# A scaled channel matmul on one core: store order, chunk sizes, weight halves, a dummy matmul loop and ScalarE as the only reader of PSUM

## The chip, the cores and the metric

The kernel runs on one core of one Trainium2 chip. The metric is device time in microseconds (us) of one execution, lower is better. Five runs of the kernel before gave 586.42 to 587.04 us, median 586.71. One more execution was taken with the hardware profiler; it took 586.91 us, and its profile covers a span of 585.1 us from the first to the last instruction.

## The reference

```python
def reference(x, dw, pw):            # x: 1 x 384 x 384 x 384 bf16; dw: 1 x 1 x 384; pw: 384 x 384
    out = x * dw[0, 0][None, None, None, :]          # k = 1: no neighbours are summed
    return jnp.einsum('bhwc,cd->bhwd', out, pw)
```

With a 1 x 1 depthwise kernel this is a single product: 147,456 pixels, each a row of 384 channels, times a 384 x 384 matrix whose rows have been scaled by `dw`. 113 MB of x are read and 113 MB of output are written, all in bf16.

## The kernel before

**Units of work.** A *supertile* is 512 pixels; there are 288 (`NS`). Supertiles are loaded and stored in *chunks* of 1 to 8 (`LMAX`), whose sizes `_chunks` (L18) lays down: 1, 1, 2, 4, then thirty-four times 8, then 4, 2, 1, 1. One supertile is 384 KB (393,216 bytes) each way; below this is called a *unit* of transfer. Three X buffers (`NX`) and three O buffers (`NO`) hold chunks in turn; T (transposed x) and PS (a PSUM tile of four banks) alternate between two buffers, by even and odd supertile.

**The steps of one supertile jj**, each on its own engine, with semaphores written out by hand:

- VectorE (DVE) turns x so that channels lie on partitions, in two 32 x 32 block transposes over uint32 (L174), one for each half of the channels. It reads x as uint32, so that two channels travel together; the weights are laid out in even and odd channels to match. From the third supertile on, each half waits until TensorE is done with the same half of supertile jj-2 (`s_pe`).
- TensorE (PE) runs 48 matmuls (L134): six blocks b of 64 channels, for each the even and the odd channel (`par`), for each four row groups q of 32 partitions, which run side by side. Call the four of one (b, par) a *group*: 12 groups to a supertile, six to each half. The first group waits for the transposes (`s_t`) and for both readers of that PSUM tile two supertiles earlier: `s_a` (ScalarE) on q = 0 and `s_d` (VectorE) on q = 3. The first group of the second half waits for the second transpose. The code is a loop of 144 rounds (L150), two supertiles to a round.
- PSUM is emptied into O as bf16 by two engines: VectorE takes the fourth bank (L212) and ScalarE (ACT) the first three (L215).

VectorE's order is: cast of jj, then the two transposes of jj+2, and so on.

**The queue of transfers.** Nearly all DMAs are issued by SyncE (SP), strictly in order: for each chunk t first the load of chunk t+3 (L95), which waits until the transposes of chunk t are done with the X buffer, then the store of chunk t (L105 to L107), which waits for both casts of its last supertile. The first eviction of a chunk waits until the store of three chunks before has left its O buffer (L210, L211).

**Before the first matmul.** SyncE and ScalarE load `pw` in four copies of 288 KB, one for each group of 32 partitions (L89). `dw` is cast by VectorE (`dwsel`, L186). Then twelve pieces w_r = pw_r times dw are made, six on VectorE (L197) and six on ScalarE (L199), and TensorE waits for all twelve (L149). VectorE transposes supertile 0 ahead of its six and supertile 1 behind them.

Of the kernel before, what the change touches and what calls it, by code (L numbers as in the profile page):

```python
# [7 lines left out]
BF16 = mybir.dt.bfloat16  # L8
F32 = mybir.dt.float32
U32 = mybir.dt.uint32  # L10
COPY = mybir.ActivationFunctionType.Copy

LMAX = 8
NX = 3
NO = 3


def _chunks(n_super: int):  # L18

    head, tail = [1, 1, 2, 4], [4, 2, 1, 1]  # L20
    mid = n_super - sum(head) - sum(tail)
    assert mid > 0 and mid % LMAX == 0
    return head + [LMAX] * (mid // LMAX) + tail
# [3 lines left out]
def kernel(  # L27
# [11 lines left out]
    nc = tc.nc  # L39
    P = nc.NUM_PARTITIONS  # L40
    B, H, W, C = x.shape
    assert dw.shape[0] == 1 and dw.shape[1] == 1, "only k=1 depthwise supported"
    D = pw.shape[1]
    N = B * H * W
    assert C == 384 and D == 384 and N % 1024 == 0
    NB = C // 64

    xf = x.rearrange("b h w c -> (b h w) c")
    of = out.rearrange("b h w d -> (b h w) d")

    NS = N // 512
    chunks = _chunks(NS)
    NT = len(chunks)
    s0 = [sum(chunks[:t]) for t in range(NT)]

    consts = ctx.enter_context(tc.tile_pool(name="consts", bufs=1))
# [3 lines left out]
    pw_r = consts.tile([P, NB, 2, D], BF16, name="pw_r")  # L60
    w_r = consts.tile([P, NB, 2, D], BF16, name="w_r")
    dwt = consts.tile([32, NB, 2], BF16, name="dwt")
    dwsel = consts.tile([P, NB * 2], F32, name="dwsel")
    warm = consts.tile([P, 3], F32, name="warm")
    seed = consts.tile([P, 2], F32, name="seed")

    Xs = [bufp.tile([P, 4 * LMAX, C], BF16, name=f"X{i}") for i in range(NX)]
    Ts = [bufp.tile([P, NB, 256], BF16, name=f"T{i}") for i in range(2)]
    Os = [bufp.tile([P, 4 * LMAX * D], BF16, name=f"O{i}") for i in range(NO)]
# [3 lines left out]
    s_t = [[nc.alloc_semaphore(f"s_t{i}{h}") for h in range(2)] for i in range(2)]  # L73
    s_pe = nc.alloc_semaphore("s_pe")
    s_a = [nc.alloc_semaphore(f"s_a{i}") for i in range(2)]
    s_d = [nc.alloc_semaphore(f"s_d{i}") for i in range(2)]
    s_o = [nc.alloc_semaphore(f"s_o{i}") for i in range(NO)]
    s_dw = nc.alloc_semaphore("s_dw")
    s_pw = nc.alloc_semaphore("s_pw")
    s_ds = nc.alloc_semaphore("s_ds")  # L80
    s_wr = nc.alloc_semaphore("s_wr")
    s_seed = nc.alloc_semaphore("s_seed")

    with tc.tile_critical():  # L84
        pw_v = pw.rearrange("(b w r) d -> w b (r d)", w=32, r=2)
        dw_v = dw.rearrange("a e (b w r) -> w (a e b) r", w=32, r=2)

        def load_pw(eng, q):
            eng.dma_start(pw_r[32 * q : 32 * q + 32].rearrange("w b r d -> w b (r d)"), pw_v).then_inc(s_pw, 16)  # L89

        def load_x(t):
            L = chunks[t]
            r = 512 * s0[t]
            src = xf[r : r + 512 * L, :].rearrange("(p s) c -> p (s c)", p=P)
            d = nc.sync.dma_start(Xs[t % NX][:, : 4 * L, :].rearrange("p s c -> p (s c)"), src)  # L95
            if t >= NX:
                je = s0[t - NX] + chunks[t - NX] - 1
                d._wait_ge(s_t[je % 2][1], je // 2 + 1)
            d.then_inc(s_x[t % NX], 16)

        def store(t):
            L = chunks[t]
            r = 512 * s0[t]
            je = s0[t] + L - 1
            nc.sync.wait_ge(s_d[je % 2], je // 2 + 2)  # L105
            dst = of[r : r + 512 * L, :].rearrange("(q p j) d -> p q (j d)", q=4, p=P)
            d = nc.sync.dma_start(dst, Os[t % NO][:, : 4 * L * D].rearrange("p (q e) -> p q e", q=4))  # L107
            d._wait_ge(s_a[je % 2], je // 2 + 2)
            d.then_inc(s_o[t % NO], 16)


        nc.scalar.dma_start(dwt[:], dw_v).then_inc(s_dw, 16)
        load_x(0)
        load_pw(nc.scalar, 2)
        load_pw(nc.sync, 0)
        load_pw(nc.scalar, 3)
        load_pw(nc.sync, 1)
        for t in range(1, NX):
            load_x(t)
        for t in range(NT):  # L120
            if t + NX < NT:
                load_x(t + NX)
            store(t)
        for o in range(NO):
            nc.sync.wait_ge(s_o[o], 16 * len(range(o, NT, NO)))


        def supertile(s, rv):
            for b in range(NB):
                for par in range(2):  # L130
                    for q in range(4):
                        if par == 0 and q == 0 and b in (0, 3):
                            nc.tensor.wait_ge(s_t[s][b // 3], rv)
                        mm = nc.tensor.matmul(  # L134
                            PS[s][:, q, :D],
                            lhsT=Ts[s][32 * q : 32 * q + 32, b, par::2],
                            rhs=w_r[32 * q : 32 * q + 32, b, par, :],
                            start=(b == 0 and par == 0),
                            stop=(b == NB - 1 and par == 1),
                            tile_position=(32 * q, 0),  # L140
                        )
                        if b == 0 and par == 0 and q == 0:
                            mm._wait_ge(s_a[s], rv)
                        elif b == 0 and par == 0 and q == 3:
                            mm._wait_ge(s_d[s], rv)
                        if b in (2, 5) and par == 1 and q == 3:
                            mm.then_inc(s_pe)

        nc.tensor.wait_ge(s_wr, 2 * NB)  # L149
        with nc.tensor.Fori(0, NS // 2, 1) as it:  # L150
            rv = nc.tensor.to_reg(it + 1)
            for s in range(2):
                supertile(s, rv)


        for s in range(2):
            nc.vector.memset(seed[:, s : s + 1], 0.0).then_inc(s_d[s])  # L157
        nc.gpsimd.memset(warm[:], 0.0).then_inc(s_seed)  # L158
        for s in range(2):
            c = nc.scalar.copy(warm[:, s + 1 : s + 2], warm[:, 0:1])  # L160
            if s == 0:
                c._wait_ge(s_seed, 1)
            c.then_inc(s_a[s])

        def transposes(t, j):
            jj = s0[t] + j
            L = chunks[t]
            s = jj % 2
            Xw = Xs[t % NX][:].bitcast(U32)[:, : 4 * L, :].rearrange("p (k l) c -> p k l c", l=L)
            Tw = Ts[s][:].bitcast(U32).rearrange("p b (i k) -> p b k i", k=4)  # L170
            for h in range(2):
                if h == 0 and j == 0:
                    nc.vector.wait_ge(s_x[t % NX], 16 * (t // NX + 1))  # L173
                ins = nc.vector.transpose(  # L174
                    out=Tw[:, 3 * h : 3 * h + 3],
                    in_=Xw[:, :, j, 96 * h : 96 * h + 96].rearrange("p k (b w) -> p b k w", w=32),
                )
                if jj >= 2:
                    ins._wait_ge(s_pe, 2 * (jj - 2) + h + 1)
                ins.then_inc(s_t[s][h])  # L180

        order = [(t, j) for t in range(NT) for j in range(chunks[t])]

        nc.vector.wait_ge(s_dw, 16)
        for q in range(4):
            nc.vector.tensor_copy(  # L186
                dwsel[32 * q : 32 * q + 32, :], dwt[:].rearrange("w b r -> w (b r)")
            ).then_inc(s_ds)
        transposes(*order[0])
        for b in range(NB):  # L190
            for r in range(2):
                eng = nc.vector if r == 0 else nc.scalar
                if b == 0:
                    eng.wait_ge(s_pw, 64)  # L194
                sc = dwsel[:, 2 * b + r : 2 * b + r + 1]
                if r == 0:
                    i = nc.vector.tensor_scalar_mul(w_r[:, b, r, :], pw_r[:, b, r, :], sc)  # L197
                else:
                    i = nc.scalar.activation(w_r[:, b, r, :], pw_r[:, b, r, :], COPY, scale=sc)  # L199
                if b == 0:  # L200
                    i._wait_ge(s_ds, 4)
                i.then_inc(s_wr)
        transposes(*order[1])

        for jj, (t, j) in enumerate(order):
            L = chunks[t]
            s = jj % 2
            Ov = Os[t % NO][:, : 4 * L * D].rearrange("p (q j d) -> p q j d", q=4, d=D)
            if j == 0 and t >= NO:
                nc.vector.wait_ge(s_o[t % NO], 16 * (t // NO))  # L210
                nc.scalar.wait_ge(s_o[t % NO], 16 * (t // NO))  # L211
            e = nc.vector.tensor_copy(Ov[:, 3, j, :], PS[s][:, 3, :D])  # L212
            e._wait_ge(s_pe, 2 * jj + 2)
            e.then_inc(s_d[s])
            a = nc.scalar.copy(Ov[:, 0:3, j, :], PS[s][:, 0:3, :D])  # L215
            a._wait_ge(s_pe, 2 * jj + 2)
            a.then_inc(s_a[s])
            if jj + 2 < NS:
                transposes(*order[jj + 2])


# [28 lines left out]
```

## Time and profile before

| what | us |
|---|---|
| median of five runs | 586.71 |
| profiled execution, and its span | 586.91, 585.1 |
| first matmul starts, last one ends | 13.48, 578.87 |
| PE busy (13,824 matmuls) | 564.1 |
| DVE busy, ACT busy | 563.9, 327.0 |
| longest wait of DVE for x once it runs | 1.6 |
| waits for a store to leave O: DVE, ACT | 2.3, 1.7 |
| bytes moved by DMA | 227.79 MB, mean 389 GB/s |

Times in a profile line are microseconds unless marked ns. A line of the timeline begins with the start and the duration, then engine, source line, operation, out<-in, and in brackets the idle time before it and what ended that. PEld is TensorE's weight load, SPq the part of SyncE that issues DMAs. "DMA" in tenths is the mean busy share of the core's 16 DMA engines in 40 slices of the span.

### The profile page before, as it was taken

How to read it: one execution, taken by the hardware profiler on the slowest of the kernel's cores; microseconds unless marked ns; L12 is line 12 of the kernel's file. 1: busy time of each engine (PE TensorE's matmuls, PEld its weight loads, DVE VectorE, ACT ScalarE, POOL GpSimd, SP SyncE). 2: the span in 40 equal slices, each digit the busy share in tenths (PEclk: the TensorE clock that was granted, in tenths of full speed). 3: DMA queues.
4: the chain of work that ended last, by engine and by line, in shares of the span. 5: the costliest groups of instructions: out<-in, count | busy, mean ns of one | idle time of the engine just before them, and what ended most of it. 6: DMA issues, size and time to landing. Idle time of an engine off the chain costs nothing.

```text
span 585.1 us, 29852 instructions
## 1 busy us (share of the span) xinstructions
PE 564.1 (96%) x13824; PEld 412.9 (71%) x13824; DVE 563.9 (96%) x876; ACT 327.0 (56%) x297; POOL 0.3 (0%) x5
## 2 busy tenths in 40 slices
PE   0999999999999999999999999999999999999995
PEld 0667777777777777777777777777777777777774
DVE  3789999999999999999999999999999999999995
ACT  3455555555555555555555555555555555555553
POOL 0000000000000000000000000000000000000000
PEclk9999999999999999999999999999999999999998
DMA  8799999999999999999999999999999999999858
GB/s 281 253 404 428 427 427 417 405 386 400 403 413 395 389 420 397 380 424 403 386 417 405 404 411 410 393 400 420 387 393 412 399 400 408 399 410 398 330 225 311
DMA packets 29277, 227.79 MB, mean 389 GB/s; under 512 B 1616, under 2 KB 5456, under 8 KB 24656
## 3 DMA queue, kind: packets, MB, share of 16 engines
q1 hardware_dynamic: 28640, 227.09, 96.9%
q10 hardware_dynamic: 624, 0.59, 0.4%
q14 instruction: 12, 0.10, 0.0%
q8 instruction: 1, 0.02, 0.0%
HBM read 114.43 MB, written 113.25 MB: 389 GB/s over the span
## 4 chain that ended last, share of the span: by engine, by line
PE 93%; DMA 5%; ACT 1%; SPq 0%; issue 0%; DVE 0%; ACTq 0%; DVEq 0%
PE ps L134 93%; DMA X<-in_x_dram 2%; DMA pw_r<-in_pw_dram 1%; DMA out_dram<-O 1%; ACT O L215 1%; ACT w_r L199 1%; DVE T L174 0%; SPq L89 0%; SPq L107 0%; SPq L95 0%; SPq L245 0%; DVEq L173 0%; ACTq L211 0%; ACTq L194 0%; SPq L84 0%
## 5 line engine op out<-in xcount | busy, mean ns | idle before, releaser
L134 PE MATMUL ps<-w_r,T 32*128 32x384 bf16 x13824 | 564.1, 322 | 14.8 <-ACT w_r L199 13.5
L134 PEld LDWEIGHTS ps<-w_r,T 32*128 32x128 bf16 x13824 | 412.9, 93 | 165.6 <-issue 15.1
L215 ACT CAST O<-ps 128x1152 bf16<-128x1152 f32 x288 | 322.3, 1119 | 245.5 <-PE ps L134 243.8
L174 DVE STREAM_TRANSPOSE T<-X 128x384 uint32<-128x384 uint32 x576 | 448.0, 850 | 1.7 <-DMA X<-in_x_dram 1.6
L212 DVE CAST O<-ps 128x384 bf16<-128x384 f32 x288 | 160.4, 557 | 7.1 <-PE ps L134 4.8
L199 ACT ACTIVATE w_r<-pw_r,dwsel 128x384 bf16<-128x384 bf16 x6 | 3.1, 602 | 6.1 <-DMA pw_r<-in_pw_dram 6.1
L186 DVE CAST dwsel<-dwt 32x12 f32<-32x12 bf16 x4 | 0.7, 164 | 4.1 <-DMA dwt<-in_dw_dram 4.0
L197 DVE TENSOR_SCALAR w_r<-pw_r,dwsel 128x384 bf16<-128x384 bf16 x6 | 1.5, 313 | 2.6 <-DMA pw_r<-in_pw_dram 2.6
L160 ACT ACT_TABLE_LOAD x1 | 1.3, 1283 | 2.3 <-issue 2.3
L157 DVE MEMSET seed<- 128x1 f32 x2 | 0.1, 59 | 1.0 <-SPq L84 1.0
L160 ACT COPY warm<-warm 128x1 f32<-128x1 f32 x2 | 0.3, 188 | 0.0
L234 POOL MEMSET const-bfloat16-1.0<- 128x1 bf16 x1 | 0.1, 102 | 0.0
L234 POOL MEMSET const-uint8-127<- 128x1 uint8 x1 | 0.1, 102 | 0.0
L158 POOL MEMSET warm<- 128x3 f32 x1 | 0.1, 101 | 0.5 <-SPq L84 0.5
L234 POOL MEMSET const-float32-0.0<- 128x1 f32 x1 | 0.1, 99 | 0.2 <-issue 0.2
L234 POOL MEMSET const-float32-1.0<- 128x1 f32 x1 | 0.1, 99 | 0.0
## 6 DMA issues: line engine op xcount, KB each, us to landing
X<-in_x_dram SPq DMA_DIRECT2D x34, 3072.0 KB, 17.8
out_dram<-O SPq DMA_DIRECT2D x34, 3072.0 KB, 23.0
X<-in_x_dram SPq DMA_DIRECT2D x2, 1536.0 KB, 12.4
out_dram<-O SPq DMA_DIRECT2D x2, 1536.0 KB, 13.6
X<-in_x_dram SPq DMA_DIRECT2D x4, 384.0 KB, 5.4
X<-in_x_dram SPq DMA_DIRECT2D x2, 768.0 KB, 10.2
out_dram<-O SPq DMA_DIRECT2D x4, 384.0 KB, 3.9
out_dram<-O SPq DMA_DIRECT2D x2, 768.0 KB, 11.3
```

What stands on the lines that cost most here:

```text
L134: mm = nc.tensor.matmul(PS[s][:, q, :D], lhsT=Ts[s][32 * q : 32 * q + 32, b, par::2], rhs=w_r[32 * q : 32 * q + 32, b, par, :], start=(b = ...
L157: nc.vector.memset(seed[:, s : s + 1], 0.0).then_inc(s_d[s])
L158: nc.gpsimd.memset(warm[:], 0.0).then_inc(s_seed)
L160: c = nc.scalar.copy(warm[:, s + 1 : s + 2], warm[:, 0:1])
L174: ins = nc.vector.transpose(out=Tw[:, 3 * h : 3 * h + 3], in_=Xw[:, :, j, 96 * h : 96 * h + 96].rearrange("p k (b w) -> p b k w", w=32),)
L186: nc.vector.tensor_copy(dwsel[32 * q : 32 * q + 32, :], dwt[:].rearrange("w b r -> w (b r)")).then_inc(s_ds)
L197: i = nc.vector.tensor_scalar_mul(w_r[:, b, r, :], pw_r[:, b, r, :], sc)
L199: i = nc.scalar.activation(w_r[:, b, r, :], pw_r[:, b, r, :], COPY, scale=sc)
L212: e = nc.vector.tensor_copy(Ov[:, 3, j, :], PS[s][:, 3, :D])
L215: a = nc.scalar.copy(Ov[:, 0:3, j, :], PS[s][:, 0:3, :D])
L234: nc = _bacc.Bacc("TRN2", target_bir_lowering=False, num_devices=1)
```

## The change

It does six things.

1. Chunk sizes: 1, 1, 2, 2, 3, 3, 4, then thirty-two times 8, then 6, 4, 3, 2, 1 (44 chunks where there were 42).
2. In every chunk of 8 with an even number, SyncE issues the store of chunk t ahead of the load of chunk t+3; elsewhere the order stays.
3. `pw` comes in eight copies of half the size, first those of blocks 0 to 2 for all four row groups, then those of blocks 3 to 5, each half with a semaphore of its own. ScalarE casts `dwsel`; VectorE makes nine of the twelve w_r pieces and ScalarE three, and TensorE waits for each piece just ahead of its use. These waits stand in the loop body, in the even supertile only: 11 groups, in all 144 rounds.
4. TensorE first runs a loop of 11 times 8 matmuls on zeros that GpSimd has written.
5. ScalarE alone empties PSUM, all four banks in one instruction. `s_d` and its waits are gone from TensorE and from the stores.
6. The last supertile is emptied by both engines, two banks each, and stored in two halves, one issued by SyncE and one by ScalarE.

```diff
-    head, tail = [1, 1, 2, 4], [4, 2, 1, 1]
+    head, tail = [1, 1, 2, 2, 3, 3, 4], [6, 4, 3, 2, 1]
...
-        def load_pw(eng, q):
-            eng.dma_start(pw_r[32 * q : 32 * q + 32].rearrange("w b r d -> w b (r d)"), pw_v).then_inc(s_pw, 16)
+        def load_pw(eng, q, h):
+            bs = slice(3 * h, 3 * h + 3)
+            eng.dma_start(
+                pw_r[32 * q : 32 * q + 32, bs].rearrange("w b r d -> w b (r d)"), pw_v[:, bs]
+            ).then_inc(s_pw[h], 16)
...
-        load_pw(nc.scalar, 2)
-        load_pw(nc.sync, 0)
-        load_pw(nc.scalar, 3)
-        load_pw(nc.sync, 1)
+        for h in range(2):
+            for q in range(2):
+                load_pw(nc.scalar, 2 + q, h)
+                load_pw(nc.sync, q, h)
...
-        for t in range(NT):
+        for t in range(NT - 1):
+            late = chunks[t] == LMAX and t % 2 == 0
+            if late:
+                store(t)
             if t + NX < NT:
                 load_x(t + NX)
-            store(t)
+            if not late:
+                store(t)
+        nc.sync.dma_start(of_last[:, 2:4], o_last[:, 2:4])._wait_ge(s_d, 1).then_inc(
+            s_last, 16
+        )
...
+        wr_eng = {(b, r): int(r == 1 and b % 2 == 0) for b in range(NB) for r in range(2)}
...
                         if b == 0 and par == 0 and q == 0:
                             mm._wait_ge(s_a[s], rv)
-                        elif b == 0 and par == 0 and q == 3:
-                            mm._wait_ge(s_d[s], rv)
+                        elif s == 0 and q == 0:
+                            mm._wait_ge(*wr_done[b, par])
...
-        nc.tensor.wait_ge(s_wr, 2 * NB)
+        nc.tensor.wait_ge(s_zero, 1)
+        with nc.tensor.Fori(0, 11, 1) as _:
+            for i in range(8):
+                nc.tensor.matmul(
+                    PS[1][:, i % 4, :D],
+                    lhsT=zero[32 * (i % 4) : 32 * (i % 4) + 32, 0:P],
+                    rhs=zero[32 * (i % 4) : 32 * (i % 4) + 32, :],
+                    start=True,
+                    stop=True,
+                    tile_position=(32 * (i % 4), 0),
+                )
+        nc.tensor.wait_ge(*wr_done[0, 0])
...
-        nc.vector.wait_ge(s_dw, 16)
+        nc.scalar.wait_ge(s_dw, 16)
...
+        for (b, r), e in wr_eng.items():
+            eng = (nc.vector, nc.scalar)[e]
+            if (e, b // 3) not in first:
+                eng.wait_ge(s_pw[b // 3], 64)
...
+            i.then_inc(s_wr[e])
...
             if j == 0 and t >= NO:
+                nc.scalar.wait_ge(s_o[t % NO], 16 * (t // NO))
+            nq = 4
+            if jj + 1 == NS:
+                nq = 2
                 nc.vector.wait_ge(s_o[t % NO], 16 * (t // NO))
-                nc.scalar.wait_ge(s_o[t % NO], 16 * (t // NO))
-            e = nc.vector.tensor_copy(Ov[:, 3, j, :], PS[s][:, 3, :D])
-            e._wait_ge(s_pe, 2 * jj + 2)
-            e.then_inc(s_d[s])
-            a = nc.scalar.copy(Ov[:, 0:3, j, :], PS[s][:, 0:3, :D])
+                e = nc.vector.tensor_copy(Ov[:, nq:4, j, :], PS[s][:, nq:4, :D])
+                e._wait_ge(s_pe, 2 * jj + 2)
+                e.then_inc(s_d)
+            a = nc.scalar.copy(Ov[:, 0:nq, j, :], PS[s][:, 0:nq, :D])
...
+        nc.scalar.dma_start(of_last[:, 0:2], o_last[:, 0:2])._wait_ge(s_a[(NS - 1) % 2], (NS - 1) // 2 + 2).then_inc(
+            s_last, 16
+        )
```

## The prediction

> **What bounds the kernel now.** I read the page's busy line and DMA line first, then the timeline of one period in mid-stream, then the chain of waits at both ends, then the DMA issues by time.
>
> ```profile
> PE 564.1 (96%) x13824; PEld 412.9 (71%) x13824; DVE 563.9 (96%) x876; ACT 327.0 (56%) x297; POOL 0.3 (0%) x5
> ...
> DMA  8799999999999999999999999999999999999858
> ```
>
> PE, DVE and the DMA engines all look full. The timeline from 301.9 us tells PE and DVE apart:
>
> ```profile
> 302.02 1.12 ACT L215 CAST O<-ps 128x1152 bf16<-128x1152 f32 x1 [0.83 <-PE ps L134]
> 302.02 0.56 DVE L212 CAST O<-ps 128x384 bf16<-128x384 f32 x1
> 302.50 1.55 DVE L174 STREAM_TRANSPOSE T<-X 128x384 uint32<-128x384 uint32 x2
> 303.97 1.12 ACT L215 CAST O<-ps 128x1152 bf16<-128x1152 f32 x1 [0.83 <-PE ps L134]
> ```
>
> A period is 303.97 - 302.02 = 1.95 us. In the matmul records the 12 groups of a supertile start 162 or 163 ns apart, with no wider gap at a supertile's border: 12 x 162.5 = 1950 ns. Both casts start together, released by PE; DVE's second transpose ends at 304.05, when PE has only begun the next supertile, whose second half is due 0.97 us later. So PE sets the pace, 288 x 1.95 = 561.6 us, and DVE's full row costs nothing. Whatever can be gained lies in the other 585.1 - 561.6 = 23.5 us. The chain shows where:
>
> ```profile
> 1.88 8.04 DMA pw_r<-in_pw_dram
> ...
> 10.01 3.15 ACT w_r L199 x6
> ...
> 13.48 4.05 PE ps L134 x48
> ...
> 19.15 12.45 DMA X<-in_x_dram
> ...
> 32.69 538.40 PE ps L134 x13248
> ...
> 572.26 7.45 DMA out_dram<-O
> ...
> 579.79 1.12 ACT O L215
> ```
>
> PE starts at 13.48; its first 14 groups are 320 ns apart (half speed, up to 17.9, where the clock record reaches 1.0), so the third supertile starts at 19.54; x is late by 1.45 us at 32.69; at the end the last cast waits for a store. The DMA engines are a second bound, close behind. This is the landing time of large DMAs at 62 to 110 us, then at 480 to 530 us:
>
> ```profile
> X<-in_x_dram SPq DMA_DIRECT2D x4, 3072.0 KB, 13.9
> out_dram<-O SPq DMA_DIRECT2D x3, 3072.0 KB, 19.2
> ```
> ```profile
> X<-in_x_dram SPq DMA_DIRECT2D x3, 3072.0 KB, 19.6
> out_dram<-O SPq DMA_DIRECT2D x3, 3072.0 KB, 25.0
> ```
>
> A DMA's semaphore is raised 16 times. The first raise stays about 10 us after the issue of a load; only the last grows, from 13.7 to 19.7. One of 16 engines falls behind: its landings are about 7.4 us apart for 8 units loaded and 8.4 for 8 stored, 15.8 in all against the 15.6 that PE takes for a chunk.
>
> **The change part by part**, as time saved or added on the path to the end.
>
> *Weights in halves (3).* In order of issue the four copies land at 6.75, 7.32, 8.82 and 9.92. The first half is the bytes of the first two, so it lands at about 7.3; the second at 9.9. X0 landed at 5.38, so DVE's transposes of supertile 0 end by 7.0. One w_r piece is 0.31 us on DVE, each further 0.245; from w_r to the first matmul took 13.48 - 13.16 = 0.32 us. PE starts at 7.3 + 0.05 + 0.31 + 0.32 = 8.0. Its six groups take 0.97; then it waits: five DVE pieces from 9.95 to 11.25, last group done at about 11.65. DVE's transposes of supertile 1 start at 11.2, the first half is ready at 12.1, PE starts it at 12.15, and the third supertile at 14.1. That is 19.5 - 14.1 = **5.4 us saved**. Between bounds: weights no earlier than now (9.9) leave a start at 10.3, a third supertile at about 14.5 and 5.0 saved; if halves cost as much as whole copies, 1.5 us less. ScalarE's four `dwsel` casts end by about 6, before any weight; its three pieces (0.52 apart) are off the path.
>
> *Dummy loop (4).* 22 groups from about 1.6 us. By the first supertile's rows, 14 at 320 ns and 8 at 162.5 are 5.8 us: done at 7.4, ahead of 8.0. All at half speed they end at 8.6, costing 0.6. Without the warm clock the head loses about 1 us. Both are in the range.
>
> The Trainium skill ("TensorE: Matmul & The Clock Gate", Part 1) gives about 3.4 us to full clock, where this trace took 4.4; its figure would end the loop at about 6.8, still ahead of the weights.
>
> *Small chunks at the head (1).* Now SyncE holds the fourth-next load (issued 19.15) behind the store of supertile 0, and 8 units then land at 31.59. After the change 3 units follow there, issued at about 13.5 and due at about 19.9; a unit takes 0.92, so they land at about 19. The next loads (3, 4, 8 units) have 3 us or more in hand. **1.45 us saved**; at worst half comes back at the first chunk of 8.
>
> *ScalarE alone (5).* 1119 ns for 1152 elements; 384 more at the nearest row's rate (about 0.83 ns) give 1.44 us, under the 1.95 period; PE needs that PSUM tile again 1.95 us after it finished it. Cover left 0.45 us. **0.** If one instruction over four banks took 1.9 us or more, each 0.1 above it would cost 29 us. DVE loses 0.48 us of work that nobody waited for, and frees X about 1 us earlier.
>
> *Eleven more waits (3).* They stand in 144 rounds. Now, the groups that carry waits (first and seventh) are spaced 162.4 to 162.6 ns like the rest, so a satisfied wait costs under 1 ns: **0**, at most 1.6 us.
>
> The Trainium skill ("Advanced Engine Details and Errata", Network/Comms) says that reading a semaphore from the sequencer takes 50 to 100 ns. If PE paid that unhidden, 1584 waits would add 79 to 158 us. The spacing above speaks against it, though only for waits at least 24 matmuls apart.
>
> *Order of transfers (2).* In even chunks the load is issued 3.4 us later and behind 8 units of store. So it lands when the store does now, 25 us after the chunk's last cast; it is needed 28.6 after. Cover 3.6 us, hence **0**; odd chunks keep their place. Fewer changes between reading and writing might help the engines; no row shows it, so -2 to +3 us, taken as 0.
>
> *Tail (1, 6).* Now PE ends at 578.9, the last store lands at 583.77, the span ends 1.36 later. Afterwards the last cast is two banks: DVE 0.16 + 768 x 1.04 ns = 0.96; two issues and hand-overs 0.5; landing 2.4 for half the bytes (2.83 now). The chunk that last used the O buffer is stored 11.7 us before PE's end, not 6.7, so that wait goes. So 3.9 instead of 4.8: **0.9 saved**, if the queue is empty.
>
> It is not quite. With PE 7 us earlier, the slow DMA engine has no idle time from 15 us on. Counting every chunk through one queue at 0.925 us a unit loaded and 1.05 stored, its last bytes land at 577 to 578.4, while PE ends at 571.9 and the tail wants 575.7. Of that excess of 1.3 to 2.7 I take about half, because the 15 other engines are quicker and DVE's halved program needs fewer of the 12 instruction fetches of 8 KB: **1.1 added**; bounds 0 and 2.7.
>
> Sum: 586.9 - 5.4 - 1.45 - 0.9 + 1.1 = 580.2 beside the profiled execution's 586.91; the median of the runs is 0.2 lower: **580.0 us**.
>
> **The rivals.**
> - *The slow DMA engine becomes the bound.* For: 15.8 against 15.6 now, and lag of 10 us at the end. At 0.93 and 1.055 a unit its queue ends at 581.2, x comes late several times near the end (the loads of the last small chunks sit behind stores of 8 units): 581.2 + 1.36 + 1.8 = **584.4**. Against: it has always caught up when demand fell.
> - *The head gains half* (clock falls back in the 1.3 us pause for the second half, or eight copies land later): 580 + 2.5 = **582.5**. Against: after the last matmul the clock stayed at 1.0 for 2.2 us.
> - *Waits in the loop hold PE up*: slower. Place: PE, even supertiles. At 10 ns each, 1584 x 10 ns = 15.8 us: 580 + 15.8 = **596**. It decides from 6.7/1584 = 4.2 ns a wait. For: one wait in every four matmuls is six times as dense as any now. Against: 162.5 ns a group gives cover, and 4 waits a supertile show nothing.
> - *ScalarE's four-bank cast is too slow*: same side, less likely.
>
> **How the numbers follow.** Differences under 0.2% (1.2 us) can't be told from no change. Forecast 0.58 (577.5 to 582), slow engine 0.19, half head 0.10, waits or cast slower 0.09, sums that cancel within 0.2% 0.04. Range 577.3 to 585.0: the low end is a tail without the 1.1 and weights 1.5 us earlier; the high end is the slow-engine case with a bit of the head lost. Faster 0.87, same 0.04, slower 0.09.
>
> **What the profile after would show.** First w_r matmul near 8.0 and third supertile near 14.1; ACT casts of 1.44 us, 1.95 apart in mid-stream (a wider period means waits or casts); no wait for x near 30; last matmul near 572; last loads landing up to 25 us after issue. I would be wrong if the period moved, if halves landed no earlier, or if PE waited for x from 500 us on.

## The result and the profile after

The changed kernel takes a median of 588.75 us against 586.42 us before; the ratio is 1.0036, 95% interval 1.0028 to 1.0045. It is slower by 0.36%, where 580.0 us, 1.1% faster, was forecast, with a range of 577.3 to 585.0. The profiled execution took 588.28 us over a span of 586.5 us (before: 586.91 and 585.1).

The page after, busy times and the group of the transposes, which are now VectorE's only steady work:

```profile
PE 570.8 (97%) x13912; PEld 418.4 (71%) x13912; DVE 496.9 (85%) x586; ACT 417.9 (71%) x298; POOL 0.5 (0%) x6
...
PE 71%; DMA 24%; DVE 2%; ACT 1%; SPq 1%; issue 0%; DVEq 0%
...
L207 DVE STREAM_TRANSPOSE T<-X 128x384 uint32<-128x384 uint32 x576 | 493.8, 875 | 80.1 <-DMA X<-in_x_dram 31.3
L250 ACT CAST O<-ps 128x1536 bf16<-128x1536 f32 x288 | 413.8, 1437 | 157.5 <-PE ps L156 157.5
```

The chain is no longer nearly all PE: 24% of it is DMA. VectorE waits 31.3 us for x, of which 5.4 are the wait for the very first chunk; the kernel before waited 1.6 once it ran. The chain in order of time (start, duration, what) shows two different halves:

```profile
2.84 6.87 DMA pw_r<-in_pw_dram
...
9.73 1.24 DVE w_r L228 x5
...
11.88 310.26 PE ps L156 x7632
...
324.06 28.38 DMA X<-in_x_dram
...
352.54 2.73 DVE T L207 x4
...
355.26 29.11 DMA X<-in_x_dram
...
385.48 31.41 PE ps L156 x768
...
418.81 29.72 DMA X<-in_x_dram
```

Up to 322 us the kernel is ahead of the one before, with an unbroken run of matmuls from 11.88. From then on x comes late in every second chunk, and five loads are on the chain; four of them took 28 to 30 us from issue to landing, the last, of 3 units, 18.5. The first late one, in the timeline:

```profile
351.41 1.44 ACT L250 CAST O<-ps 128x1536 bf16<-128x1536 f32 x1 [0.51 <-PE ps L156]
352.54 5.06 DVE L207 STREAM_TRANSPOSE T<-X 128x384 uint32<-128x384 uint32 x7 [2.20 <-DMA X<-in_x_dram]
353.36 1.44 ACT L250 CAST O<-ps 128x1536 bf16<-128x1536 f32 x1 [0.51 <-PE ps L156]
...
353.55 3.76 PE L156 MATMUL ps<-w_r,T 32*128 32x384 bf16 x88 [0.24 <-DVE T L207]
...
355.73 1.44 ACT L250 CAST O<-ps 128x1536 bf16<-128x1536 f32 x1 [0.93 <-PE ps L156]
```

VectorE stands still for 2.20 us until x lands, and the casts are 355.73 - 353.36 = 2.37 us apart instead of 1.95. From the matmul records, the supertiles longer than 1950 ns, beyond that length, are: 0.42 us at 351, 0.73 at 383, 1.03 at 415, 0.74 at 447, 1.51 at 479, 0.76 at 512, 2.18 at 563; and 0.88 and 0.81 at 567 and 570, where the clock record has fallen to 0.5 for 3.4 us after that pause of 2.2 us. Seven waits cost 7.4 us, the clock 1.7.

The books close: third supertile at 13.83 instead of 19.54 (-5.7), the early wait for x gone (-1.45), waits +7.4, clock +1.7, and from PE's last matmul to the end 5.8 instead of 6.3 us (-0.5). That is +1.4 us, and 586.5 - 585.1 = 1.4.

Why do the loads take so long? Landing times of the 3 MB transfers at 62 to 110 us, then at 300 to 350:

```profile
out_dram<-O SPq DMA_DIRECT2D x3, 3072.0 KB, 14.2
X<-in_x_dram SPq DMA_DIRECT2D x3, 3072.0 KB, 20.9
```
```profile
X<-in_x_dram SPq DMA_DIRECT2D x3, 3072.0 KB, 25.0
out_dram<-O SPq DMA_DIRECT2D x3, 3072.0 KB, 28.1
```

The lines for X mix turned and other loads. A load that is turned behind a store started with 20.9 us, but takes 28.4 by 324 us, where its cover (28.6 from the chunk's last cast) is used up. The first raise of a DMA's semaphore does not move: for the late loads it stays at 16.1 to 16.3 us after the issue, from 100 us to 500. Only the last of the 16 drifts, from 4 us behind the eighth to 14, while the fifteenth stays within 2 us of the eighth. So one DMA engine lags, as before the change, but its lag grows faster.

### The profile page after: what moved, and what is told of

It is laid out like the page before. It is cut to its first block, busy times and chain, and to the rows that moved or that the text cites. A ratio compares the mean times of both kernels' runs of the same rounds, so it can differ in the third digit from the quotient of the medians.

```text
span 586.5 us, 29841 instructions
## 1 busy us (share of the span) xinstructions
PE 570.8 (97%) x13912; PEld 418.4 (71%) x13912; DVE 496.9 (85%) x586; ACT 417.9 (71%) x298; POOL 0.5 (0%) x6
## 4 chain that ended last, share of the span: by engine, by line
PE 71%; DMA 24%; DVE 2%; ACT 1%; SPq 1%; issue 0%; DVEq 0%
PE ps L156 71%; DMA X<-in_x_dram 23%; DVE T L207 1%; DMA pw_r<-in_pw_dram 1%; ACT O L250 1%; SPq L113 0%; SPq L92 0%; DVE w_r L228 0%; DVE O L247 0%; SPq L100 0%; DVEq L206 0%; SPq L283 0%; SPq L86 0%
## 5 line engine op out<-in xcount | busy, mean ns | idle before, releaser
L207 DVE STREAM_TRANSPOSE T<-X 128x384 uint32<-128x384 uint32 x576 | 493.8, 875 | 80.1 <-DMA X<-in_x_dram 31.3
L250 ACT CAST O<-ps 128x1536 bf16<-128x1536 f32 x288 | 413.8, 1437 | 157.5 <-PE ps L156 157.5
L175 PE MATMUL ps<-zero 32*128 32x384 bf16 x88 | 5.5, 423 | 1.4 <-POOL zero L191 1.4
L175 PEld LDWEIGHTS ps<-zero 32*128 32x128 bf16 x88 | 3.0, 117 | 3.5 <-issue 1.6
L230 ACT ACTIVATE w_r<-pw_r,dwsel 128x384 bf16<-128x384 bf16 x3 | 1.7, 610 | 2.6 <-DMA pw_r<-in_pw_dram 2.6
```

The source lines that it names most:

```text
L175: nc.tensor.matmul(PS[1][:, i % 4, :D], lhsT=zero[32 * (i % 4) : 32 * (i % 4) + 32, 0:P], rhs=zero[32 * (i % 4) : 32 * (i % 4) + 32, :], s ...
L207: ins = nc.vector.transpose(out=Tw[:, 3 * h : 3 * h + 3], in_=Xw[:, :, j, 96 * h : 96 * h + 96].rearrange("p k (b w) -> p b k w", w=32),)
L250: a = nc.scalar.copy(Ov[:, 0:nq, j, :], PS[s][:, 0:nq, :D])
```

## The experiments

Three theories stood. **G (grouping):** store, store, load, load in a row makes the lagging engine slower. **L (late load):** the engine is as it was, the turned loads just go out too late. **E:** something else in the change, ScalarE's eviction or the chunk sizes, slows it. "Two chunks" below is the mean time between landings on the lagging engine for 16 units loaded and 16 stored; PE needs 31.2 us for them. "Lag" is the time from the eighth to the sixteenth raise of one DMA's semaphore. All ratios are to the kernel before on the same chip, with their 95% intervals; runs 1 to 4 share one chip, 5 to 8 a second, 9 and 10 a third. Numbers other than times and ratios come from the one profiled execution of each run.

**1. The changed kernel with the old order.**

```diff
-            late = chunks[t] == LMAX and t % 2 == 0
+            late = False
```

> The changed kernel with the old order of transfers in every chunk (load, then store); all else as changed. Theory G (grouping): two stores and then two loads in a row make the lagging DMA engine slower, 32.1 us for two chunks instead of about 31.5; without it the lag stays as in the kernel before, no wait for x after 350 us, 579 to 581.5 us. Theory L (late load): the engine's rate has nothing to do with the order; the loads of even chunks are just issued too late; also 579 to 581.5, but the lagging engine still takes about 32 us for two chunks and the lag still grows past 10 us. Theory E (ScalarE's eviction or the chunk sizes slow the DMA): the lag grows as in the changed kernel and waits for x come, only later; 583 to 587.

Measured: 578.90 us, ratio 0.9877 (0.9862 to 0.9892). No supertile after the second is longer than 1.95 us; two chunks take about 31.4 us; the lag stays at 9 us or less. The landing times at 400 to 500 us:

```profile
out_dram<-O SPq DMA_DIRECT2D x7, 3072.0 KB, 23.1
X<-in_x_dram SPq DMA_DIRECT2D x6, 3072.0 KB, 18.8
```

That is 588.75 - 578.90 = 9.9 us for one line (9.3 by the two ratios), as much as the whole miss of the forecast (588.75 - 580.0 = 8.75). E is out.

**2. Every chunk of 8 with the store first.**

```diff
-            late = chunks[t] == LMAX and t % 2 == 0
+            late = chunks[t] == LMAX
```

> The changed kernel with the store ahead of the load in every chunk of 8, so that stores and loads alternate one by one again, but every load is as late as the late ones are now. Theory G: the lagging engine returns to about 31.5 us for two chunks, a load lands about 25 us after its issue at the end, under its 28.6 us of cover: 579.5 to 582. Theory L: twice as many late loads, so waits for x in every chunk: 590 or more. Theory E: as the changed kernel, 588 to 592.

Measured: 578.62 us, ratio 0.9872 (0.9857 to 0.9887), the shortest median here, though not to be told from run 1. Twice as many late loads, and not one wait for x reaches PE. Landing times at 400 to 500 us:

```profile
out_dram<-O SPq DMA_DIRECT2D x7, 3072.0 KB, 15.4
X<-in_x_dram SPq DMA_DIRECT2D x7, 3072.0 KB, 22.9
```

Two chunks take 31.3 to 31.4 us, the lag is at most 7 us. L is out: a load behind a store is harmless when stores and loads alternate.

**3. The changed kernel with four X buffers.**

```diff
-NX = 3
+NX = 4
```

> The changed kernel with four X buffers instead of three: a load has one more chunk (15.6 us) until it is needed. Theory G: the lag goes on growing by about 0.9 us for two chunks, no wait for x, but at the end the lagging engine still has some 15 us of stores and loads to work off: 581 to 584. Theory L: no waits and no growth, 579 to 581. Theory E: like G.

Measured: 583.75 us, ratio 0.9958 (0.9945 to 0.9972). No wait for x in mid-stream, yet two chunks take 32.1 to 32.3 us and the lag reaches 15.5: the drift is there without the waits. The time itself has another part that no theory named (us in total, times, longest; the profiled execution, at 585.09, was the slowest of five):

```profile
ACT O L250 <- PE ps L156: 148.4, 282, 2.1
...
ACT O L250 <- DMA out_dram<-O: 6.8, 3, 3.1
```

With four buffers the loads run further ahead at the head, so the first stores queue behind 8-unit loads, ScalarE waits there twice for O (2.6 and 3.1 us), and PE loses 5.9 us between 35 and 54 us (about 1.7 of it to 3.4 us at half clock). The third wait for O, at 501 us, costs PE 0.3 us. More cover moved the wait from x to O.

**4. The kernel before with only the order turned.**

```diff
+            late = chunks[t] == LMAX and t % 2 == 0
+            if late:
+                store(t)
             if t + NX < NT:
                 load_x(t + NX)
-            store(t)
+            if not late:
+                store(t)
```

> The kernel before with only the order of transfers turned in every even chunk of 8. Theory G: the lagging engine goes from 31.5 to about 32.1 us for two chunks, loads land over 28 us after issue from about 350 us on, waits for x of about 0.9 us every second chunk: 590 to 595. Theory L: late loads with a lag that grows as before, one or two short waits near the end: 586.5 to 588.5. Theory E: 586 to 587, since nothing else of the change is in.

Measured: 595.83 us, ratio 1.0161 (1.0147 to 1.0174), just over the range of G. Two chunks take 32.3 us, the first wait for x in mid-stream comes at 358 us, then one of about 1.0 us in every second chunk, and one of 3.4 us at 581:

```profile
DVE T L178 <- DMA X<-in_x_dram: 10.8, 7, 3.6
PE ps L138 <- DVE T L178: 9.4, 8, 3.2
```

Price of the order here: 595.83 - 586.01 (before, same chip) = 9.8 us, the same as in experiment 1.

**5. and 6. Smaller chunks: how long may a run one way be?** Chunks of at most 4 with six buffers each, the order turned in 5 and old in 6.

```diff
-LMAX = 8
-NX = 3
-NO = 3
+LMAX = 4
+NX = 6
+NO = 6
...
-    head, tail = [1, 1, 2, 2, 3, 3, 4], [6, 4, 3, 2, 1]
+    head, tail = [1, 1, 2, 2, 3, 3, 4], [4, 4, 3, 2, 2, 1]
```

> The changed kernel with chunks of at most 4 and six X and six O buffers, order still turned in every even full chunk: stores and loads come two by two again, but a run of the same kind is 8 units long, as in the kernel before, not 16. Theory R (what slows the lagging engine is a run of 16 units one way; its lag can grow until it stands half a period behind the others): lag settles near 8 to 10 us, about 31.5 us for 16 units each way, no wait for x, 578 to 580.5 us. Theory P (the pairing itself, two stores and two loads in a row, whatever their size): lag grows on as in the changed kernel, but cover is longer by two small chunks; 581 to 588.

> The same with the old order, so a run one way is 4 units long. Theory R: lag settles at about 4 to 6 us, 578 to 580 us. Theory P: lag as in the kernel before, 10 us at the end, 578 to 580.

Measured: turned 578.98 us (ratio 0.9870, 0.9845 to 0.9896) with a lag of up to 11.6 us; old 583.84 us (0.9956, 0.9927 to 0.9985; single runs 581.6 to 587.0) with a lag of 13 us. The first fits R, with a lag a little over its figure. The second lies outside both theories, which gave 578 to 580, and refutes R as stated: runs of 4 units should have had the least lag and have more than runs of 8 (16 units each way take 31.8 us on the lagging engine in run 6, 31.6 in run 5). In the profile of run 6, of one of its two fastest executions (581.63), no supertile after the first is longer than 1.95 us; what is left over runs after PE's last matmul at 571.5 (end 579.8). So of the sizes tried "a pair is bad" holds for chunks of 8 only, and the length of a run alone does not tell the lag.

**7. and 8. The price of the chunk sizes and of the dummy loop**, both on the version with the old order: in 7 the sizes of the kernel before, in 8 the loop of 11 times 8 matmuls taken out.

```diff
-    head, tail = [1, 1, 2, 2, 3, 3, 4], [6, 4, 3, 2, 1]
+    head, tail = [1, 1, 2, 4], [4, 2, 1, 1]
```

> The changed kernel with the old order and with the old chunk sizes, to price the new sizes alone against the run with the old order (578.9). By the prediction's terms: x of the first chunk of 8 late by about 1.2 us near 24 us, and the last cast waiting for a store near the end by about 0.9: 580 to 582. If the sizes are hidden by other work: 578.5 to 579.5.

> The changed kernel with the old order and without the dummy matmul loop. By the rows of the first supertile before (320 ns a group for 4.4 us), the second half of supertile 0 and a little of supertile 1 run at half speed: third supertile at 14.4 to 14.8 instead of 14.0, 579.3 to 580. If the pauses for the weights keep the clock down longer: third supertile at 16 or later, 580.5 to 582. If the loop is worth nothing: 578.9.

Measured: old sizes 580.68 us (0.9900, 0.9874 to 0.9927); no loop 578.94 (0.9872, 0.9846 to 0.9898). With the old sizes a supertile at 23 us is 1.74 us too long and the last cast waits for a store again:

```profile
DVE T L207 <- DMA X<-in_x_dram: 10.8, 4, 5.2
DVE O L247 <- DMA out_dram<-O: 2.6, 1, 2.6
```

The sizes are worth 1.3 us by the ratios (0.9900 against 0.9877 of run 1, on another chip) and 1.7 against run 8 on the same chip, inside what was expected. No worth of the loop shows, to within the intervals of about 1.5 us, and the head agrees: without it the third supertile starts at 13.66, with it at 14.04. The clock then reaches full speed at 11.0, and the half-speed groups of supertile 0 fall into the time in which PE would have waited for the second half of the weights.

**9. Pairs made the other way round**: load, load, store, store, no load late, four O buffers.

```diff
-            late = chunks[t] == LMAX and t % 2 == 0
-            if late:
-                store(t)
+            held = chunks[t] == LMAX and chunks[t + 1] == LMAX and t % 2 == 0
             if t + NX < NT:
                 load_x(t + NX)
-            if not late:
-                store(t)
+            if held:
+                continue
+            if t and chunks[t - 1] == LMAX and chunks[t] == LMAX and t % 2 == 1:
+                store(t - 1)
+            store(t)
```

> The changed kernel with pairs made the other way: in two chunks of 8 SyncE issues load, load, store, store, so that no load is late (each goes out as soon as its X buffer is free) and four O buffers give the held-back stores room. Theory G (pairs slow the lagging engine by 0.7 us in one load of two): 31.9 to 32.2 us for two chunks and a lag that grows past 12 us, although no load is issued late; x still in time or late only near the end, work left over in the tail: 580 to 586. Theory L (only the late issue of loads matters): about 31.4 us for two chunks, lag under 10 us, 578.5 to 580.

Measured: 593.69 us, ratio 1.0132 (1.0115 to 1.0149), worse than either theory said. Two chunks take about 32.5 us over 140 to 500 us, and the lag reaches 18 us. Late x costs PE 5.6 us from 413 to 563 us; after 569 us three more supertiles, of the last small chunks, are 6.9 us too long in all, with the clock at half from 574 to 581. Landing times at 400 to 500 us:

```profile
out_dram<-O SPq DMA_DIRECT2D x7, 3072.0 KB, 37.3
X<-in_x_dram SPq DMA_DIRECT2D x6, 3072.0 KB, 30.0
```

Loads that go out in time are late all the same. Pairs of 8 units are enough.

**10. The kernel before with the store first in every chunk of 8.**

```diff
-            late = chunks[t] == LMAX and t % 2 == 0
+            late = chunks[t] == LMAX
```

(Against experiment 4.)

> The kernel before with the store ahead of the load in every chunk of 8. Theory G: one by one again, so the lagging engine keeps about 31.4 us for two chunks, the lag stays under 9 us and no wait for x comes in mid-stream: 585 to 587. Theory L: every load is late, waits for x in every chunk of the last third: over 592.

Measured: 587.84 us, ratio 1.0032 (1.0015 to 1.0049), 0.8 above G's range. Two chunks take 31.4 us, the lag stays at 6 us, and in mid-stream nothing waits for x. What is lost is one wait of 2.0 us at the end, where the load of a small chunk sits behind a store of 8 units:

```profile
572.29 0.56 DVE L216 CAST O<-ps 128x384 bf16<-128x384 f32 x1
575.02 1.54 DVE L178 STREAM_TRANSPOSE T<-X 128x384 uint32<-128x384 uint32 x2 [2.17 <-DMA X<-in_x_dram]
```

**What G looks like inside.** The table gives the time between the landings of successive 8-unit transfers issued at 200 to 330 us (of pairs, the whole pair), in us, from the semaphore raises in the traces: the 16th raise is the lagging engine, the 8th an ordinary one.

| kernel | lagging: store | lagging: first, second load of a pair (or each load) | lagging: two chunks | ordinary: loads |
|---|---|---|---|---|
| before | 8.4 | 7.45 | 31.7 | 8.0 |
| old order (1) | 8.4 | 7.3 | 31.3 | 7.85 |
| store first everywhere (2) | 8.4 | 7.2 | 31.2 | 7.4 |
| changed | 8.4 | 7.9, 7.3 | 32.0 | 7.3, 8.2 |
| before, turned (4) | 8.4 | 8.2, 7.3 | 32.3 | 7.4, 8.1 |
| load, load, store, store (9) | 8.4 | 8.5, 7.3 | 32.6 | 7.2, 9.2 |

The lagging engine's stores always take 8.4 us (an ordinary engine's 7.4 to 7.5 where they were issued well ahead); that is not the change. In the last column the 9.2 of run 9 contains waiting for the issue. What the pairs add is 0.6 to 1.2 us in one load of two. On ordinary engines the load with a store queued right behind it takes 8.0 to 8.2 instead of 7.3: in the changed kernel's packet records loads of 24 KB take 912 ns, but 1.2 to 1.7 us on average from 251 to 253 us, just before these engines turn to stores. In run 1 and in the kernel before, the lagging engine is by then some 5 to 8 us behind and mostly in a store, and loses little (at 124, 235 and 251 us single loads of the kernel before take 7.9 to 8.0). In the changed kernel it is in a load: the second of the pair while its lag is under 7 us (landings at 127 to 167 us: first 7.2, second 8.0 and 8.4), the first once the lag is over 8 (7.9, 7.3). This fits the rows with chunks of 8. That it is the cause is inferred from the times, no run changed this alone, and run 6, where 4-unit runs should have settled early, speaks against its simplest form. What stays open is why runs of 4 lag more, and why this one engine's stores are slower.

## Why the prediction was wrong, step by step

- **Weights in halves:** right. First matmul at 8.05 (8.0 forecast), third supertile at 13.83 (14.1), 5.7 us saved against 5.4.
- **Dummy loop:** it ended at 6.9 (7.4). The statement that the head loses 1 us without it fell: in run 8 the third supertile starts 0.4 us earlier without it, and the time is the same.
- **Small chunks at the head:** right, no wait for x reaches PE before 350 us; 1.45 us saved.
- **ScalarE alone:** right, 1437 ns against 1.44 us (0.83 ns for each of the 384 more elements, as assumed), period still 1.95.
- **Eleven more waits:** right. In the changed kernel's trace the groups of the even supertile that carry a wait start 162 or 163 ns apart like all others. The 50 to 100 ns for reading a semaphore of the Trainium skill ("Advanced Engine Details and Errata", Network/Comms) do not show on PE at this density either.
- **Tail:** 0.5 saved instead of 0.9 in the changed kernel, where the lagging engine still has work; the last two halves land 2.95 and 3.38 us after issue, not 2.4. In run 1 the halves take 2.7 and 3.0, and from PE's last matmul to the end it is 5.4 us instead of 6.3: the 0.9 is there. The 11.7 and 6.7 us that were compared are not alike, since the first leaves out the cast before the store; in run 1 that store goes out 10.2 us before PE's end.
- **Order of transfers, taken as 0:** this is the step that failed. It measured +9.9 us (run 1), against bounds of -2 to +3. A turned load was given about 25 us to land, with 28.6 until it is needed; in the changed kernel it took 20.9 us at 74 us, 25.1 at 199 and 28.4 at 324, and was late from there on. What was wrong was to take the landing time of the kernel before, and with it the lagging engine's rate of 0.925 and 1.05 us a unit, as given. In the runs the rate goes with the order: with the turned pairs the mean load takes 7.6 to 7.7 us for 8 units, not 7.3 to 7.45, so that two chunks take 32.0 to 32.3 us and not 31.3 to 31.7, where PE needs 31.2; at 0.9 us for each, the eight pairs from 74 to 324 us use up the cover.
- **Slow engine, 1.1 us added, and the rival "the slow DMA engine becomes the bound" at 584.4:** the 1.1 does not show. In run 1 PE ends at 571.9, as reckoned, the lagging engine has caught up by the last stores, and 578.9 is 1.1 below the forecast. The rival named the right place, x late because one engine lags, but expected it only near the end and at an unchanged rate; in the changed kernel it came from 350 us on, through the order. Also missing was the clock: a pause of 2.2 us late in the stream cost another 1.7 us.

## What to carry to other kernels

When DMA and the bounding engine need nearly the same time per period, look at the last of the 16 landings and not at the mean share: here an engine that lost 0.1 to 0.5 us in two chunks was harmless over the whole stream, and one that lost 0.9 us was not. A new order of transfers has then to be priced by its rate over the whole stream, not by the slack of one load. Here, with the rest of the change in, alternating stores and loads one by one, whichever goes first, gave 578.6 to 578.9 us; turned pairs of 3 MB cost 9.8 and 9.9 us in the two kernels. The changed kernel with either alternating order beats both the kernel before and the changed one as it stands.

## What the runs showed of the hardware

- One of the 16 DMA engines is slower in stores, 8.4 us for 8 units against 7.4 to 7.5. It is so while the others store (80 us in the changed kernel) and while they load; then, at 241 to 247 us, only its own 6 KB packets are in the records, and they take about 267 ns on average, where 234 is the usual. Such an engine lags in every run here, on three chips; which of the 16 it is, the records do not tell.
- PE's clock fell to half after a pause of 2.2 us in the changed kernel (565 us) and of 2.3 us in run 3 (47 us), but not after 2.0 us in run 10 (572 us) nor 3.4 us in run 4 (581 us). So the length of a pause alone does not decide; where it lies does. In all twelve traces the stretches between two changes of the clock are whole multiples of 3.413 us (in run 3: 13, 1 and 155 of them). Laid on this grid, the full clock was halved at the end of every step in which PE had no matmul for 2.0 us or more, and after none with 1.9 us or less: the pause of the changed kernel lies in one step, that of run 4 is split into 1.35 and 1.88 us (without a matmul; the pauses above are what the supertile gained, up to 0.2 us more). The Trainium skill ("TensorE: Matmul & The Clock Gate", "Why this matters for your kernels") warns of gaps over about 3 us; here shorter ones were enough. Part 1 of the same page says that the window in which activity is counted runs freely, and the grid in these traces agrees with that. Full speed came 4.4 us (before), 3.7 us (changed) and 3.1 us (run 8) after the first matmul, around the 3.4 us that Part 1 gives.
